# Softmax maxima transposed in place, and a new order of all engines, in a four-layer decode kernel

## The chip, the cores and the metric

The kernel runs on one core of a Trainium2 chip. The metric is the device time of one execution in microseconds (us). Lower is better.

## What is computed

Eight sequences (B = 8) decode one token each. Four layers follow one another: attention (A), MLP (B), attention, MLP, each with a layernorm ahead and a residual sum behind. Both attention layers use the same weights and the same cache.

```python
def _A_ref(x, k_cache, v_cache, wq, wo):         # Hq 16, Hkv 8, Dh 256
    q = (x @ wq).reshape(B, Sq, Hq, Dh)          # D = 448
    k, v = the last W = 1024 rows of each cache, each head used by two query heads
    scores = einsum("bhqd,bhkd->bhqk", q, k) * Dh ** -0.5
    return (einsum("bhqk,bhkd->bhqd", softmax(scores), v)) @ wo
def _B_ref(x, w1, w2):                           # F = 1792
    return silu(x @ w1) @ w2
x = A_x
x = x + _A_ref(_layernorm(x), A_k_cache, A_v_cache, A_wq, A_wo)
x = x + _B_ref(_layernorm(x), B_w1, B_w2)
x = x + _A_ref(_layernorm(x), A_k_cache, A_v_cache, A_wq, A_wo)
x = x + _B_ref(_layernorm(x), B_w1, B_w2)
```

K and V of a sequence are 8 blocks of 512 KB each, so 8.4 MB per sequence and 67 MB in all. The weights add some 10 MB.

## The kernel before

**Work.** A "batch" b is one sequence. `layer1(b)` is its first attention ("layer 0" in the names: S0, PV0). `layer2(b)` is `chain(b)` (layernorm, w1, tanh, w2, fold, layernorm, wq, query blocks) and then its second attention ("layer 1": S1, PV1). The wo of the second attention and the last MLP are done for all eight batches at once, in `final_wo` and `final_rows`.

**Scores and softmax.** A K block that has landed is transposed in place by VectorE, in 32-bit words, two instructions for each slot (L947). `scores` makes 64 matmuls for half the heads (k2 = 0 or 1), and a VectorE reduction (L650) leaves the negated maxima in column k2 of `mseg`. `softmax` combines the maxima of a group of 32 partitions: a transpose (L656), a minimum (L657), and a transpose back (L660) into the same memory as `mseg`, which is called `mb` there. ScalarE makes the exponentials (L664) with these as bias. TensorE transposes them (L669), ScalarE copies them (L673), and the P V products follow (L701, and L731 for the last head of layer 0). Before the change the first transpose wrote `mT`, one tile for both layers. `mseg`, `mg` and `mb` exist once for each layer.

**Slots.** 30 slots of 512 KB hold K and V blocks in turn; a batch takes 16 of them. A K slot comes free when S1 of its half is done, a V slot when PV1 has used it. `pump` adds the loads in the order K 0 to 7, V 0 to 7, batch after batch, all on the SP queue (L471 for K, L477 and L483 for V). Load i reuses the slot of load i - 30: V blocks 6 and 7 of batch b take the slots of K blocks 0 and 1 of batch b - 1.

**Order.** `add` records each task with the keys that it reads and writes. A task that writes a key depends on the last writer and on all readers since, in the order in which the program adds the tasks. `schedule` then makes one fixed order for each engine. A task's urgency is its rank, the length of the remaining path in us by the planner's costs, plus a bias for its kind:

```python
part = "e" if prio < 0 or prio >= 9000 else "abc"[(prio % 100 >= 60) + (prio % 100 >= 70)]
self.kind = ".".join([eng, *(p for i, p in enumerate(name.split(".")) if i != 1), part])
urgency = [t.rank + BIAS.get(t.kind, 0.0) for t in tasks]
sooner = [u for u in can if urgency[u.idx] > urgency[t.idx] and at(u) < now + HOLD * occ[t.idx]]
```

So "pe.S0.1.a" is the second half of layer 0's scores, ".a" is `layer1`, ".b" is `chain` with S1, ".c" is the second attention's softmax and all after it, and ".e" is the start and `final_rows`. `HOLD` says how long an engine is held for a more urgent task that isn't ready yet; `PE_SCALE` multiplies the costs of TensorE tasks. At run time each engine takes its instructions in this order, with semaphore waits where a dependency crosses engines.

**Fillers.** `keep` (L777) and `idle` (L784) are matmuls with zero weights, added to a bank without changing it.

Of the kernel before, what the change touches and what calls it, by code (L numbers as in the profile page):

```python
# [5 lines left out]
F32 = mybir.dt.float32  # L6
U32 = mybir.dt.uint32
ALU = mybir.AluOpType
ACTF = mybir.ActivationFunctionType
AX = mybir.AxisListType  # L10
# [12 lines left out]
       "act:exp": 0.38, "act:oev": 0.30, "act:pTev": 0.20, "act:qrow": 0.51, "act:rowb": 0.50, "act:tanh": 0.22,  # L23
       "pool:pow": 0.53, "pool:pow8": 1.63}
SP_ISSUE, DMA_FIRST, DMA_LAST = 0.47, 1.2, 2.2
HOLD, PE_SCALE = 0.837, 1.062
BIAS = {"dve..e": -51.1, "pe.qsel1.a": -37.9, "pe.S0.0.a": -128.5, "act.exp.a": -58.6, "pe.l.a": 18.8, "act..a":
        -106.8, "act.oev.a": -58.1, "pe.oT.a": 43.2, "pe.wo.a": -42.9, "pe.stat.b": 263.8, "pe.qturn.b": 188.6,
        "pe.qsel.b": 262.3, "dve.max.b": 218.8, "dve.mT.c": 118.3, "dve.mg.c": 108.3, "dve.mb.c": 87.2,
        "act.pTev.c": -93.6, "act.oev.c": -59.6, "pe.oT.c": -79.9, "pe.PV1.1.0.c": -83.7, "pe.PV1.1.2.c":  # L30
        -139.0, "pe.PV1.1.3.c": -36.7, "pe.wo8.c": -95.5, "pe.idle.e": -7.4, "dve.nm8.e": -11.1, "pe.xres.e":
        -10.8}


class Task:
# [13 lines left out]
class Plan:  # L49
# [10 lines left out]
    def add(self, eng, fns, reads=(), writes=(), dur=0.1, prio=0.0, name="", n_bytes=0, dma_key=None):  # L60
        if not isinstance(fns, (list, tuple)):
            fns = [fns]
        if eng == "pool":
            writes = list(writes) + ["pool_serial"]
        t = Task(eng, list(fns), dur, prio, name, n_bytes)
        t.idx = len(self.tasks)
        t.sem = dma_key
        deps = {}

        def dep(o, raw):  # L70
            if o is not t:
                deps[o.idx] = (o, raw or (deps[o.idx][1] if o.idx in deps else False))

        for k in reads:
            if k in self.last_w:
                dep(self.last_w[k], True)
            if k[0] == "bank":
                for r in self.readers.get(k, ()):
                    if r.eng != eng:
                        dep(r, False)  # L80
        for k in writes:
            if k in self.last_w:
                dep(self.last_w[k], True)
            for r in self.readers.get(k, ()):
                dep(r, False)
        for k in reads:
            if k not in writes:
                self.readers.setdefault(k, []).append(t)
        for k in writes:
            self.last_w[k] = t  # L90
            self.readers[k] = []
        t.deps = deps
        self.tasks.append(t)
        return t

    def schedule(self):
# [15 lines left out]
        for t in reversed(tasks):  # L112
            r = max([u.rank + lag(t, u, raw) for u, raw in succ[t.idx]], default=0.0)
            t.rank = occ[t.idx] + r
            if t.eng == "sp":
                t.rank += DMA_FIRST + DMA_LAST
                if t.idx in following:
                    t.rank = max(t.rank, occ[t.idx] + following[t.idx].rank)
        urgency = [t.rank + BIAS.get(t.kind, 0.0) for t in tasks]

# [132 lines left out]
def bass_interleave_layers__sliding_block_cached__dense_activation_silu__decode_kernel(  # L253
# [9 lines left out]
    P = 128  # L263
# [15 lines left out]
    sb = nc.alloc_sbuf_tensor  # L279
# [18 lines left out]
    e_sb = [qbd[i][:].rearrange("p (a b) c d -> p a (b c d)", a=2).rearrange("p a (u n) -> p a u n", u=2) for i in range(2)]  # L298
    pT_sb = [sb(f"pT_sb{i}", [P, 4, 32], BF16) for i in range(2)]
    mseg = [sb(f"mseg{i}", [P, 32], F32) for i in range(2)]  # L300
    mT = [sb("mT", [P, 32], F32)] * 2
    mg = [sb(f"mg{i}", [P, 2], F32) for i in range(2)]
    mb = mseg
    l_sb = [sb(f"l_sb{i}", [P, H], F32) for i in range(2)]
# [42 lines left out]
    def bk(i):  # L347
        return [("bank", i)]
# [4 lines left out]
    def dve(fn, reads, writes, dur, prio, name=""):  # L353
        add("dve", fn, reads=reads, writes=writes, dur=max(0.06, dur - LAT["dve"]), prio=prio, name=name)

    def act(fn, reads, writes, dur, prio, name=""):
        add("act", fn, reads=reads, writes=writes, dur=dur - LAT["act"], prio=prio, name=name)

    def pe(fns, reads, writes, shape, prio, name=""):

        n = len(fns) if isinstance(fns, (list, tuple)) else 1
        add("pe", fns, reads=reads, writes=writes, dur=n * max(0.0265, shape[0] / shape[1] / 2230.0), prio=prio,
            name=name)
# [289 lines left out]

    def softmax(b, layer, prio):
        sc, lb, ei = SC[layer], LB[layer], layer
        dve(lambda e: e.transpose(mT[ei][:], mseg[ei][:]), [("mseg", ei), ("mseg", ei, 0), ("mseg", ei, 1)], ["mT"], 0.21, prio, "mT")  # L656
        dve(lambda e: e.tensor_reduce(  # L657
            mg[ei][:], mT[ei][:, 0:8].rearrange("p (q r) -> p r q", r=2), AX.X, ALU.min),
            ["mT"], [("mg", ei), "mT"], 0.16, prio, "mg")
        dve(lambda e: e.transpose(mb[ei][:].rearrange("p (q r) -> p q r", r=2),  # L660
                                  mg[ei][:].unsqueeze(1).broadcast_to([P, 16, 2])),
            [("mg", ei)], [("mseg", ei), ("mseg", ei, 0), ("mseg", ei, 1)], 0.19, prio, "mb")
        for k2 in range(2):
            act(lambda e, k2=k2: e.activation(  # L664
                e_sb[ei][:, k2, :, :].rearrange("p uh (jj ul) -> p uh jj ul", ul=4),
                bank[sc][:, k2 * 256:(k2 + 1) * 256].rearrange("p (ul uh jj) -> p uh jj ul", ul=4, uh=2),
                ACTF.Exp, bias=mb[ei][:, k2:k2 + 1], scale=1.0),
                bk(sc) + [("mseg", ei, k2)], [("qbd", ei, k2)], 0.5, prio, "exp")
        pe([lambda e, c=c: e.matmul(  # L669
            bank[lb][:].bitcast(BF16)[:, c * P:(c + 1) * P], e_sb[ei][:, c // 2, c % 2, :], ident[:, :],  # L670
            is_transpose=True, start=True, stop=True) for c in range(4)],
           [("qbd", ei, 0), ("qbd", ei, 1), "ident"], bk(lb), (P, 1), prio, "pT")
        act(lambda e: e.activation(  # L673
            pT_sb[ei][:].rearrange("p c (j r) -> p c j r", j=4),
            bank[lb][:].bitcast(BF16)[:, 0:512].rearrange("p (c j r) -> p c j r", c=4, j=4)[:, :, :, 0:8], ACTF.Copy),
            bk(lb), [("pT", ei)], 0.3, prio, "pTev")
        pe([lambda e, uh=uh: e.matmul(  # L677
            bank[lb][:, C_L:C_L + 64], ones_b,
            pT_sb[ei][:].rearrange("p (k uh) n -> p uh k n", uh=2)[:, uh, :, :],
            start=(uh == 0), stop=(uh == 1)) for uh in range(2)],  # L680
           [("pT", ei), "ones_b"], bk(lb), (64, 1), prio, "l")
        dve(lambda e: e.tensor_reduce(  # L682
            l_sb[ei][:], bank[lb][:, C_L:C_L + 64].rearrange("p (n q r) -> p n r q", q=4, r=2), AX.X, ALU.add),
            bk(lb), [("l", ei), ("rl", ei)], 0.23, prio, "lsum")
        dve(lambda e: e.reciprocal(rl_sb[ei][:], l_sb[ei][:]), [("l", ei)], [("l", ei), ("rl", ei)], 0.25, prio, "rl")
# [252 lines left out]
    def layer1(b):  # L938
        prio = 100 * b + 50
        qi = 0  # L940
        if b == 0:
            q_blocks1(0, prio - 45)
        for k in range(8):
            s = slot_of[b, "k", k]
            for h in range(2):
                v = slots[s][:, h * 1024:(h + 1) * 1024].bitcast(U32)
                dve(lambda e, v=v: e.transpose(v, v), [("slot", s)], [("slot", s)], 0.67, prio, "KT")  # L947
        for k2 in range(2):
            scores(b, 0, qi, k2, prio)
        softmax(b, 0, prio)  # L950
        x_init(b, prio)
        if b == 0:
            row_sums(w2_sb, "w2", [(0, 4), (4, 7), (7, 11), (11, 14)], 40)
            row_sums(wo_sb, "wo", [(0, 5), (5, 8), (8, 13), (13, 16), (16, 21), (21, 24), (24, 29), (29, 32)], 40)
        pv_rows(b, 0, 0, prio, oT1, "oT1")
        if b > 0:
            idle(4, prio, "s1", XB)
        wo_part(b, (0, 1), 7, prio + 1)
        wo_part(b, (2, 3), 7, prio + 1)
        pv_rows(b, 0, 1, prio, oT1, "oT1", 3)  # L960
        wo_part(b, (4, 5, 6), 7, prio)
        pv_cols(b, 0, 7, prio, oT1, "oT1")
        wo_part(b, (7,), 7, prio)
        fold(prio, 1.0, [])
        if b + 1 < NB:
            q_blocks1(b + 1, prio + 1)

    def layer2(b):
        prio = 100 * b + 60
        chain(b, prio)  # L970
        for k2 in range(2):
            scores(b, 1, 1, k2, prio + (0.5 if k2 == 0 else 1))
            freed.update((b, "k", 4 * k2 + j) for j in range(4))
            pump()
        prio = 100 * b + 170
        softmax(b, 1, prio)
        if b == NB - 1:
            idle(5, prio, "s1", SC[0])
        for k2 in range(2):
            pv_rows(b, 1, k2, prio + 2, oT2[:, :, :, b], ("oT2", b))  # L980
            freed.update((b, "v", 4 * k2 + q) for q in range(4))
            pump()
            if b == NB - 1:
                final_wo(k2, prio + 3)
# [37 lines left out]
```

## Time and profile before

| | |
|---|---|
| median of 13 runs | 259.0 us (257.02 to 262.48) |
| the profiled execution | 258.75 us, of which its span is 256.5 us |
| busy in the span | PE 191.2, PEld 102.3, DVE 152.6, ACT 88.3, POOL 11.8 us |
| queue of all loads (q1) | 77.68 MB in 50192 packets |
| granted TensorE clock | 0.967 (mean) |

The span goes from the first to the last instruction of the program. PE is TensorE's matmuls, PEld its weight loads, which overlap them; DVE is VectorE, ACT ScalarE, POOL GpSimd, and SP the engine that issues the loads. A busy PE is not PE at its peak, and a DMA engine that is busy need not move data at its full rate.

### The profile page before, as it was taken

The page shows a single profiled execution, that of the slowest core. Times are in us where ns is not written, and L with a number is a line of the kernel's source. Part 1 is how long each engine was busy: PE and PEld are TensorE (multiplying, and loading weights), DVE is VectorE, ACT ScalarE, POOL GpSimd, SP SyncE. Part 2 cuts the span into 40 slices and gives each one's busy share as a digit, 9 for nine tenths or more (in the row PEclk, how much of TensorE's full clock was granted, in tenths as well). Part 3 has the DMA queues.
Part 4 walks back from the last instruction along what each step waited for, and adds up shares of the span by engine and source line. Part 5 has one row for each costly group of instructions (what it writes and reads, how often), then busy time and mean ns, then how long its engine had stood idle before and what let it go on. Part 6 is the DMA issues. An engine that isn't in the chain of part 4 may idle for free.

```text
span 256.5 us, 8596 instructions
## 1 busy us (share of the span) xinstructions
PE 191.2 (75%) x3820; PEld 102.3 (40%) x3820; DVE 152.6 (59%) x416; ACT 88.3 (34%) x241; POOL 11.8 (5%) x25
## 2 busy tenths in 40 slices
PE   0050241388869888998799799979987899798796
PEld 0050120043445345545444454545454445443453
DVE  6448675916872895587488548647853785221322
ACT  2000374815223523432453235334424431423112
POOL 1200000000000000000000000000000000000000
PEclk9999995569999999999999999999999999999999
DMA  6999999999999999999999899989999998300000
GB/s 232 355 383 380 297 341 347 348 362 396 374 350 390 401 351 360 406 375 329 388 406 350 290 403 388 348 245 399 383 324 319 414 360 275 118 3 0 3 3 4
DMA packets 50228, 78.22 MB, mean 305 GB/s; under 512 B 2304, under 2 KB 41104, under 8 KB 49808
## 3 DMA queue, kind: packets, MB, share of 16 engines
q1 hardware_dynamic: 50192, 77.68, 87.1%
q8 instruction: 30, 0.49, 0.8%
q14 instruction: 6, 0.05, 0.1%
HBM read 77.67 MB, written 0.01 MB: 303 GB/s over the span
## 4 chain that ended last, share of the span: by engine, by line
PE 48%; SPq 20%; DMA 13%; DVE 8%; ACT 6%; issue 2%; POOL 0%; ACTq 0%; DVEq 0%
DMA slot<-in_A_k_cache_dram 13%; PE bank L643 11%; PE bank L701 8%; SPq L483 6%; PE bank L818 5%; SPq L433 5%; PE bank L777 4%; PE bank L770 4%; SPq L471 3%; SPq L477 3%; ACT qbd L664 3%; DVE mseg L650 3%; PE bank L805 2%; DVE slot L947 2%; PE bank L521 2%
## 5 line engine op out<-in xcount | busy, mean ns | idle before, releaser
L947 DVE STREAM_TRANSPOSE slot<-slot 128x512 uint32<-128x512 uint32 x128 | 82.4, 686 | 13.5 <-DMA slot<-in_A_k_cache_dram 13.2
L701 PE MATMUL bank<-slot,pT_sb 128*2 128x256 bf16 x960 | 38.2, 279 | 9.5 <-DMA slot<-in_A_v_cache_dram 9.1
L643 PE MATMUL bank<-slot,qbd 128*8 128x256 bf16 x1024 | 39.4, 282 | 4.8 <-DVE mseg L650 2.5
L701 PEld LDWEIGHTS bank<-slot,pT_sb 128*2 128x2 bf16 x960 | 20.4, 83 | 18.6 <-DMA slot<-in_A_v_cache_dram 9.0
L664 ACT ACTIVATE qbd<-bank,mseg 128x256 bf16<-128x256 f32 x32 | 13.0, 473 | 41.6 <-DVE mseg L660 22.4
L643 PEld LDWEIGHTS bank<-slot,qbd 128*8 128x8 bf16 x1024 | 21.0, 85 | 13.1 <-DVE mseg L650 4.5
L709 ACT ACTIVATE qbd<-bank 128x256 bf16<-128x256 f32 x32 | 12.3, 384 | 24.7 <-PE bank L701 18.9
L612 ACT ACTIVATE qbd<-bank,mask 128x128 bf16<-128x128 f32 x32 | 12.1, 378 | 24.8 <-PE bank L607 23.6
L770 PE MATMUL bank<-wo_sb,oT 128*1 128x449 bf16 x256 | 19.6, 359 | 0.0
L777 PE MATMUL bank<-wq_sb,cols_b 128*128 128x512 bf16 x64 | 19.4, 384 | 0.0
L755 POOL TENSOR_TENSOR rhalf<-var,nhalf 128x1 f32<-128x1 f32 x16 | 8.8, 550 | 217.0 <-ACT var L753 217.0
L650 DVE TENSOR_REDUCE mseg<-bank 128x1 f32<-128x256 f32 x32 | 12.9, 414 | 8.6 <-PE bank L643 8.3
L818 PE MATMUL bank<-wq_sb,xbt 128*1 128x512 bf16 x256 | 16.6, 378 | 0.6 <-DVE xbt L744 0.6
L669 PE MATMUL bank<-ident,qbd 128*128 128x128 bf16 x64 | 6.4, 222 | 13.8 <-ACT qbd L664 13.8
L715 DVE TENSOR_TENSOR oT<-bank,l_sb 128x16 bf16<-128x16 f32 (+1 forms) x32 | 5.9, 199 | 16.7 <-PE bank L711 16.3
L682 DVE TENSOR_REDUCE l_sb<-bank 128x16 f32<-128x64 f32 x16 | 3.2, 201 | 19.3 <-PE bank L677 19.3
L784 PE MATMUL bank<-wq_sb,cols_b 128*128 128x512 bf16 x49 | 13.5, 382 | 0.0
L825 ACT ACTIVATE qrow<-bank 128x512 bf16<-128x512 f32 x16 | 9.6, 597 | 9.1 <-PE bank L818 9.1
L669 PEld LDWEIGHTS bank<-ident,qbd 128*128 128x128 bf16 x64 | 3.6, 98 | 19.2 <-ACT qbd L664 19.2
L452 DVE TENSOR_REDUCE qbd<-wo_sb 128x5 f32<-128x2240 bf16 x4 | 9.7, 2480 | 2.6 <-DMA wo_sb<-in_A_wo_dram 2.6
L626 DVE TENSOR_TENSOR qbd<-bank,maskr 128x256 bf16<-128x256 f32 x16 | 6.8, 424 | 6.8 <-PE bank L621 6.7
L790 ACT ACTIVATE qrow<-bank 128x449 bf16<-128x449 f32 x8 | 4.4, 550 | 17.7 <-PE bank L770 17.7
(146 smaller groups left out, 214.4 us busy)
## 6 DMA issues: line engine op xcount, KB each, us to landing
slot<-in_A_k_cache_dram SPq DMA_DIRECT2D x64, 512.0 KB, 10.6
slot<-in_A_v_cache_dram SPq DMA_DIRECT2D x64, 512.0 KB, 8.8
wo_sb<-in_A_wo_dram SPq DMA_DIRECT2D x1, 3584.0 KB, 17.8
wq_sb<-in_A_wq_dram SPq DMA_DIRECT2D x3, 1024.0 KB, 7.1
w_sb<-in_B_w_dram SPq DMA_DIRECT2D x4, 336.0 KB, 16.2
w_sb<-in_B_w_dram SPq DMA_DIRECT2D x1, 1344.0 KB, 11.3
wq_sb<-in_A_wq_dram SPq DMA_DIRECT2D x2, 256.0 KB, 10.5
w_sb<-in_B_w_dram SPq DMA_DIRECT2D x4, 112.0 KB, 9.4
```

Of the source, the lines that this page charges most:

```text
L433: dma(lambda e, j=j: e.dma_start(rows[:, 3 * j:3 * j + 3, :], parts[j, 0:3 * P, :].rearrange("(c p) n -> p c n", p=P)), [("w2", j)], 3 * P ...
L483: dma(lambda e: e.dma_start(slots[s][:, :].rearrange("v (j n) -> v j n", j=4), src.rearrange("j (v uh) d -> v j (uh d)", uh=2)), [("slot", ...
L643: fns.append(lambda e, cb=cb, par=par, j=j, kvh=kvh, kv=kv: e.matmul(bank[sc][32 * j:32 * j + 8, k2 * 256:(k2 + 1) * 256], qbd[qi][:, kvh, ...
L650: dve(lambda e: e.tensor_reduce(mseg[layer][:, k2:k2 + 1], bank[sc][:, k2 * 256:(k2 + 1) * 256], AX.X, ALU.max, negate=True), bk(sc), [("m ...
L664: act(lambda e, k2=k2: e.activation(e_sb[ei][:, k2, :, :].rearrange("p uh (jj ul) -> p uh jj ul", ul=4), bank[sc][:, k2 * 256:(k2 + 1) * 2 ...
L701: fns.append(lambda e, q=q, uh=uh, j=j, vv=vv: e.matmul(bank[ob][32 * j:32 * j + 2, c0:c0 + DH], pT_sb[ei][:, k2 * 2 + uh, j * 8 + 2 * q:j ...
L709: act(lambda e: e.activation(o_t, bank[ob][:, c0:c0 + DH], ACTF.Copy), bk(ob), [("qbd", ei, k2)], 0.42, prio, "oev")
L770: fns.append(lambda e, i=i, c=c, kvh=kvh: e.matmul(bank[XB][32 * c:32 * c + 1, 0:D1], oT1[:, i % 2, i // 2:i // 2 + 1], wo_sb[:, i * DP:i ...
L777: pe([lambda e: e.matmul(bank[SC[1]][:], zero_b.broadcast_to([P, P]), wq_sb[:, 0:512], start=False, stop=True, skip_group_check=True) for ...
L784: pe(lambda e: e.matmul(bank[bi][:], zero_b.broadcast_to([P, P]), wq_sb[:, 0:512], start=False, stop=True, skip_group_check=True), [("wq", ...
L818: pe([lambda e, j=j, c=c, k2=k2, wb=wb: e.matmul(bank[wb][32 * j:32 * j + 1, :], xbt[:, xcol(c, k2):xcol(c, k2) + 1], wq_sb[:, c * HD + (( ...
L947: dve(lambda e, v=v: e.transpose(v, v), [("slot", s)], [("slot", s)], 0.67, prio, "KT")
```

## The change

The tile `mT` is gone. The first transpose of `softmax` works in place in `mseg[ei]`, the minimum reads it there, and the second transpose writes back into it as it did before. All three carry the keys of their own layer's `mseg`, so no key is shared by the softmaxes of the two layers. The constants that shape the order of all engines are new.

```diff
-HOLD, PE_SCALE = 0.837, 1.062
-BIAS = {"dve..e": -51.1, "pe.qsel1.a": -37.9, "pe.S0.0.a": -128.5, "act.exp.a": -58.6, "pe.l.a": 18.8, "act..a":
-        -106.8, "act.oev.a": -58.1, "pe.oT.a": 43.2, "pe.wo.a": -42.9, "pe.stat.b": 263.8, "pe.qturn.b": 188.6,
-        "pe.qsel.b": 262.3, "dve.max.b": 218.8, "dve.mT.c": 118.3, "dve.mg.c": 108.3, "dve.mb.c": 87.2,
-        "act.pTev.c": -93.6, "act.oev.c": -59.6, "pe.oT.c": -79.9, "pe.PV1.1.0.c": -83.7, "pe.PV1.1.2.c":
-        -139.0, "pe.PV1.1.3.c": -36.7, "pe.wo8.c": -95.5, "pe.idle.e": -7.4, "dve.nm8.e": -11.1, "pe.xres.e":
-        -10.8}
+HOLD, PE_SCALE = 0.435, 1.148
+BIAS = {"pe.S0.0.a": 21.5, "dve.max.a": 23.0, "pe.S0.1.a": 61.5, "dve.mg.a": 3.5, "dve.mb.a": -28.7,
+        "dve.rsum.a": 92.7, "pe.PV0.0.0.a": -48.9, "act.oev.a": -15.0, "dve.oTev.a": 22.4, "dve.xb.b": 37.0,
+        "pe.stat.b": 20.8, "pe.w1.b": 12.9, "pe.keep.b": -26.6, "pe.w2.b": 19.7, "pe.fold.b": 57.4,
+        "pe.qturn.b": 40.0, "pe.qsel.b": 62.1, "pe.S1.0.b": 37.2, "dve.max.b": 26.6, "pe.PV1.0.1.c": -60.2,
+        "pe.PV1.1.0.c": -70.8, "pe.PV1.1.3.c": -28.5, "pe.idle.a": 36.6}
...
-    mT = [sb("mT", [P, 32], F32)] * 2
...
-        dve(lambda e: e.transpose(mT[ei][:], mseg[ei][:]), [("mseg", ei), ("mseg", ei, 0), ("mseg", ei, 1)], ["mT"], 0.21, prio, "mT")
+        M = [("mseg", ei), ("mseg", ei, 0), ("mseg", ei, 1)]
+        dve(lambda e: e.transpose(mseg[ei][:], mseg[ei][:]), M, M, 0.21, prio, "mT")
         dve(lambda e: e.tensor_reduce(
-            mg[ei][:], mT[ei][:, 0:8].rearrange("p (q r) -> p r q", r=2), AX.X, ALU.min),
-            ["mT"], [("mg", ei), "mT"], 0.16, prio, "mg")
+            mg[ei][:], mseg[ei][:, 0:8].rearrange("p (q r) -> p r q", r=2), AX.X, ALU.min), M, [("mg", ei)] + M, 0.16, prio,
+            "mg")
         dve(lambda e: e.transpose(mb[ei][:].rearrange("p (q r) -> p q r", r=2),
                                   mg[ei][:].unsqueeze(1).broadcast_to([P, 16, 2])),
-            [("mg", ei)], [("mseg", ei), ("mseg", ei, 0), ("mseg", ei, 1)], 0.19, prio, "mb")
+            [("mg", ei)], M, 0.19, prio, "mb")
```

## The prediction

> **What bounds the kernel now.** I read the slices of the page first, then the chain, then the waits of the DMA queue, then one batch in the stretches and in the timeline.
>
> ```profile
> DMA  6999999999999999999999899989999998300000
> GB/s 232 355 383 380 297 341 347 348 362 396 374 350 390 401 351 360 406 375 329 388 406 350 290 403 388 348 245 399 383 324 319 414 360 275 118 3 0 3 3 4
> PE 48%; SPq 20%; DMA 13%; DVE 8%; ACT 6%; issue 2%; POOL 0%; ACTq 0%; DVEq 0%
> SPq L477 <- PE bank L643: 28.4, 7, 5.5
> ```
>
> The loads run until slice 34 (about 221 us); then 35 us follow without any. The DMA row says 9 nearly throughout, yet the second line dips once per batch (290, 245, 319) and touches 414: the engines are occupied, not full. The last line says why: seven times the SP queue stood with a V load until score matmuls (L643) gave a slot back.
>
> The trace's landing of each load gives the prices: in a full queue a K load lands 1.28 us after the one before it, a V load 1.47 us. A batch of 8 + 8 therefore costs 8 x 1.28 + 8 x 1.47 = 22.0 us. The first K load of batches 2 to 7 landed at 82.16, 104.24, 127.61, 150.92, 175.32 and 200.19, the last V load at 221.5. From 82.16 the pure stream would need 6 x 22.0 - 1.28 = 130.7 us and end at 212.9; so 8.6 us are lost to slots that come late. Now the loop that makes them late:
>
> ```profile
> 143.90:167.63 23.73, 21.45 (x439) 11.55 (x439) 15.63 (x43) 8.95 (x24) 1.10 (x2) 1.00 1.01 359
> 221.50:256.50 35.00, 30.43 (x588) 15.30 (x580) 8.67 (x40) 9.31 (x24) 1.65 (x3) 1.00 0.01 3
> 143.41 0.75 DVE L650 TENSOR_REDUCE mseg<-bank 128x1 f32<-128x256 f32 x2 [0.17 <-PE bank L643]
> 143.89 1.15 PE L643 MATMUL bank<-slot,qbd 128*8 128x256 bf16 x32 [0.17 <-DVE mseg L650]
> 145.09 0.42 DVE L650 TENSOR_REDUCE mseg<-bank 128x1 f32<-128x256 f32 x1 [0.93 <-PE bank L643]
> 145.55 0.21 DVE L656 STREAM_TRANSPOSE mT<-mseg 128x32 f32<-128x32 f32 x1
> 145.79 0.16 DVE L657 TENSOR_REDUCE mg<-mT 128x2 f32<-128x8 f32 x1
> 145.99 0.21 DVE L660 STREAM_TRANSPOSE mseg<-mg 128x32 f32<-128x32 f32 x1
> 146.12 0.17 DVE L656 STREAM_TRANSPOSE mT<-mseg 128x32 f32<-128x32 f32 x1
> 146.29 1.57 ACT L664 ACTIVATE qbd<-bank,mseg 128x256 bf16<-128x256 f32 x4 [4.82 <-DVE mT L656]
> 149.01 1.48 PE L701 MATMUL bank<-slot,pT_sb 128*2 128x256 bf16 x48
> ```
>
> The first two lines are one steady batch and the tail (columns: PE, PEld, DVE, ACT, POOL busy, clock, DMA share, GB/s). A batch takes 23.73 us at full clock; PE is busy in 21.45 of them, of which 12 fillers (`keep` L777, `idle` L784) hold about 3.0, each counted to the next matmul's start.
>
> In the timeline, the two L650 at 143.41 are the first half of layer 1 of batch 3 and the second half of layer 0 of batch 4: the latter's maxima are complete at 144.16. The matmuls at 143.89 and the L650 at 145.09 are layer 1's second half. Only then comes an L656, and only after its L657 the other L656. In program order `softmax(3, 1)` is added before `softmax(4, 0)`, and both write "mT": the planner must put layer 1's transpose and minimum first. So batch 4 waits from 144.16 to 146.12 for the end of batch 3, and its two exponentials are third and fourth of the four from 146.29. This sits on the loop: softmax(4, 0), P V, wo, both halves of the MLP, wq, scores of layer 1, and again the same.
>
> **What the Trainium skill says.** "PSUM — Partial Sum Buffer", Engine vs sequencer instructions: the queues of ScalarE and VectorE are strict FIFO, and matmuls start and complete in program order. The trace agrees: VectorE has only 0.75 us of work between 143.41 and 145.09 and doesn't take the ready L656. "DMA: Bandwidth & Descriptors", Anatomy of one DMA: the DMA engines wait for no semaphore; the issuing sequencer does. The L477 waits above are that. "Perfetto Trace Analysis", Optimization Strategy: a gap that repeats can mean too few buffers; here 30 slots for 16 loads a batch, and the gap repeats.
>
> **The change, part by part.**
> - *Tile and in-place transpose.* The same three VectorE instructions per softmax, 16 times: 0.21 + 0.16 + 0.21 us; none added, no DMA or POOL work moves. In-place 32-bit transposes already run at L947 (686 ns for 128x512, x128), so I book no difference; bounds, from the 0.17 to 0.21 of L656: -0.04 to +0.04 us each, under 0.7 us in all.
> - *What falls away.* Layer 0's transpose can start at 144.2, its exponential 0.64 us later at 144.9 instead of 147.03 (146.29 plus two exponentials at 0.37): 2.1 us. The transposes (L669), P V of layer 0 at 149.01 and wo after it move by the same, or more if the score matmuls of the next batch are put earlier. That shortens the loop from 23.73 to about 21.6.
> - *What is late next.* The stream at 22.0 us a batch, and PE. The V loads 6 and 7 also form a loop: V7 of batch 5 was issued at 167.55, when S1 of batch 4 freed its slot, landed at 174.06, and the column P V needing it began at 176.57, 14.3 us before the next S1 half ended. That is 6.5 + 14.3 = 20.8 without slack, under the stream. PE has 21.45 us of work per batch; its busiest share in any batch stretch is 91%. At 95% the period is 22.6 us. I take 22.6: bounds 22.0 (the stream) and 23.6 (21.45 at 91%).
> - *The new order* (HOLD 0.837 to 0.435, PE_SCALE, BIAS). A bias is in us of remaining path, and one batch is 23.7. S0.1 gets +61.5 and S0.0 goes from -128.5 to +21.5: scores of the next layer 0 come before most of chain(b), whose steps carry 12.9 to 62.1. PV1.1 stays negative (-28.5 to -70.8), PV0.0.0 gets -48.9: these fill PE's gaps. That uses the new freedom; its cost is in the rivals. Unshown by the trace: I book zero apart from the period, bounds -1 to +1 us a batch. The tail's own biases (`.e`) go: 30.43 of 35.00 us are busy PE there, so zero, bounds -0.7 to +0.7.
> - *Sum.* Six batch steps from batch 1's to batch 7's layer-1 scores. Five at 23.7 - 22.6 = 1.1 make 5.5; the last, without loads to wait for, gets 1.0, half of the 2.1. The tail from V7 of batch 7 on keeps its length, as its P V (221.21) already started within 0.3 us of the last landing. 6.5 us off the profiled time of 258.75 (span 256.5 + 2.25 around it) is 252.25; the median of the 13 runs is 0.25 higher: **252.4**.
> - *Ends.* All 8.6 us of the stream, plus 1.0 in the last step: 249.4; with the small terms (0.6 and 0.7) on the good side 248. At 23.6 a batch, with the last step's 1.0: 257.4.
>
> **Rivals.**
> 1. *PE crowded (slower).* What may now be queued ahead of chain(b): S0.1 (1.1 us), the transposes (0.4), P V of layer 0 (1.8), four `idle` (1.0): 4.3 us. PE is FIFO; if a score group at the head waits for a late K transpose (L947 waited 13.2 us for loads in all), fold, w1, w2 and wq stand behind it, and behind S1 the SP queue. The slack from 20.8 to 23.73 is 2.9 us; above that the kernel gets slower. With 3.8 of it in the way, 0.9 x 6 = 5.4 us: 264. For it: 21.45 busy of 23.73. Against: S0 is already interleaved with the chain, and 3.0 us are fillers.
> 2. *Slots, not softmax (no change).* If the new order leaves S1's first half no earlier, V6 and V7 land as before, only 2.5 us (174.06 to 176.57) before they are needed, and the gain is eaten: 258.9. For it: that thin margin. Against: S1 follows the loop that gets shorter.
> 3. *The freedom is not used.* If VectorE's new order still has layer 1's softmax first, the time is 258.8. `mb` of layer 0 at -28.7 and the missing lift of layer 1's steps speak for and against.
>
> **How the numbers follow.** About 0.3% is what a measurement of this kernel can tell from no change: 258.2 to 259.8. Main case, 248 to 254.5: 0.50; a part of it, 254.5 to 258.2: 0.17; rivals 2 and 3: 0.08; rival 1, from 259.8 to 268: 0.25. Range: 5% lies below 248 and some 14% of rival 1 above 262.
>
> **What would show it.** Right: an L656 and its L660 well before layer 1's last L650 of the batch, layer 0's exponentials apart from layer 1's; batch stretches of 22 to 23 us; first K landings 22.0 to 22.8 apart; no slice under 320 GB/s between 59 and 210 us; the last V load at 213 to 217. Wrong: stretches of 24 us or more with PE waiting at L643 for VectorE's slot transposes (rival 1), or V loads still issued one S1 late with the softmaxes apart (rival 2).

## The result, and the profile after

| | before | changed |
|---|---|---|
| median | 259.36 us (48 runs) | 254.2 us (11 runs, 252.61 to 256.48) |
| the profiled execution | 258.75, span 256.5 | 255.35, span 253.5 |
| mean granted clock in it | 0.967 | 0.979 |

The ratio is 0.9803, with a 95% interval of 0.9777 to 0.983: about 5 us less. The two profiled spans differ by only 3.0 us; the changed one's profile is 1.15 us above its median. In this text a *step* is the time from the end of the first half of layer 1's scores of one batch to the same point of the next. (A correction to the description above: the scores of one half are 32 matmuls, not 64; both halves together are 64.)

From the page of the changed kernel, the slices (clock, DMA share, bandwidth):

```profile
PEclk9999999999777999999999999999999999999999
DMA  6999999999999999999999999999999999100000
GB/s 227 366 389 380 308 342 348 348 371 393 376 350 386 378 322 319 393 392 349 355 407 373 337 377 408 349 356 402 384 339 381 398 354 320 57 3 3 0 3 5
```

And its chain by engine:

```profile
PE 55%; SPq 16%; DMA 9%; DVE 8%; ACT 6%; issue 3%; POOL 0%; ACTq 0%; DVEq 0%
```

The dips of the GB/s line to 290 and 245 are gone, the last V load lands at 217.83 us instead of 221.5, and more of the chain is PE (55%, 48% before). A second profile of the same kernel, reported below, is less clear in both: one slice at 279 GB/s, and 50% of the chain on PE. The clock line shows what I hadn't reckoned with: slices 11 to 13 run below full clock.

One batch in the timeline of the changed kernel, with VectorE, ScalarE and TensorE in one list (start, us, engine, line, operation):

```profile
142.05 0.42 DVE L648 TENSOR_REDUCE mseg<-bank 128x1 f32<-128x256 f32 x1 [0.62 <-PE bank L641]
142.51 0.21 DVE L655 STREAM_TRANSPOSE mseg<-mseg 128x32 f32<-128x32 f32 x1
142.76 0.16 DVE L656 TENSOR_REDUCE mg<-mseg 128x2 f32<-128x8 f32 x1
...
142.96 0.21 DVE L659 STREAM_TRANSPOSE mseg<-mg 128x32 f32<-128x32 f32 x1
...
143.26 0.84 ACT L663 ACTIVATE qbd<-bank,mseg 128x256 bf16<-128x256 f32 x2 [1.83 <-DVE mseg L659]
...
144.16 0.40 PE L668 MATMUL bank<-ident,qbd 128*128 128x128 bf16 x4 [0.29 <-ACT qbd L663]
...
144.48 1.09 PE L641 MATMUL bank<-slot,qbd 128*8 128x256 bf16 x32
...
145.63 0.42 DVE L648 TENSOR_REDUCE mseg<-bank 128x1 f32<-128x256 f32 x1 [1.30 <-PE bank L641]
146.08 0.21 DVE L655 STREAM_TRANSPOSE mseg<-mseg 128x32 f32<-128x32 f32 x1
...
146.53 1.04 PE L700 MATMUL bank<-slot,pT_sb 128*2 128x256 bf16 x32
...
146.83 0.84 ACT L663 ACTIVATE qbd<-bank,mseg 128x256 bf16<-128x256 f32 x2 [1.96 <-DVE mseg L659]
```

Layer 0 of batch 4 has its last maximum at 142.47 and is transposed at once (142.51). Its exponentials are finished before the last score matmuls of batch 3's layer 1 (144.48) begin. Layer 0's first P V of batch 4 follows the end of those by 0.96 us; before the change it was 3.98. Layer 1's own softmax starts later, at 146.08, and nothing waits for it. The in-place transpose takes 0.21 us in all 16 cases.

The steps of the changed kernel from batch 3 to 4 and from 5 to 6 (columns as in the prediction):

```profile
142.94:165.07 22.13, 21.16 (x440) 11.62 (x440) 15.95 (x42) 9.12 (x24) 1.10 (x2) 1.00 1.05 370
...
188.01:211.87 23.86, 21.26 (x441) 11.76 (x441) 15.89 (x42) 9.24 (x24) 1.10 (x2) 1.00 1.05 370
```

PE's work per step is nearly what it was, 21.2 us, in 22.13 us instead of 23.7: 96% busy. The second stretch is the worst of the six. The mean of the six is 22.66 us here and 22.90 in the second profile, so one profile gives a step to about a quarter of a microsecond.

TensorE's own waits show what the tie cost. Both lines are of the window from 143 to 165 us, the first before the change and the second after it (who waited for whom; us in total, times, longest):

```profile
PE bank L669 <- ACT qbd L664: 1.5, 2, 1.2
PE bank L668 <- ACT qbd L663: 0.3, 1, 0.3
```

Over the six steps TensorE stood 0.9 to 1.5 us for the exponentials before and stands 0.3 to 0.4 us now: in the mean 1.0 us less, where the step is 1.2 us shorter. The 3.98 us between the scores and layer 0's first P V were thus mostly not idle. Fillers, two groups of transposes and some of layer 1's P V stood in them, and this work is now elsewhere in the step.

**Where the 3.0 us of the two profiles come from**, by the same four points in both traces:

| stretch | before | changed | difference |
|---|---|---|---|
| start to batch 1's first S1 half | 95.69 | 98.02 | +2.33 |
| six steps to batch 7's | 143.12 | 135.94 | -7.18 |
| from there to the last VectorE operation | 15.86 | 16.55 | +0.69 |
| writing the output, to the end | 1.86 | 2.97 | +1.11 |

### The profile page after: what moved, and what is told of

It reads as the page before. It is cut to its first block, busy times and chain, and to the rows that moved or that the text cites. A ratio compares the mean times of both kernels' runs of the same rounds, so it can differ in the third digit from the quotient of the medians.

```text
span 253.5 us, 8598 instructions
## 1 busy us (share of the span) xinstructions
PE 194.2 (77%) x3820; PEld 104.6 (41%) x3820; DVE 153.4 (61%) x416; ACT 89.1 (35%) x241; POOL 11.8 (5%) x25
## 4 chain that ended last, share of the span: by engine, by line
PE 55%; SPq 16%; DMA 9%; DVE 8%; ACT 6%; issue 3%; POOL 0%; ACTq 0%; DVEq 0%
PE bank L641 11%; PE bank L700 10%; SPq L481 6%; PE bank L817 6%; DMA slot<-in_A_v_cache_dram 6%; PE bank L769 5%; SPq L431 5%; PE bank L776 4%; DMA slot<-in_A_k_cache_dram 4%; ACT qbd L663 3%; PE bank L804 2%; DVE mseg L648 2%; PE bank L519 2%; DVE slot L946 2%; SPq L469 2%
## 5 line engine op out<-in xcount | busy, mean ns | idle before, releaser
L946 DVE STREAM_TRANSPOSE slot<-slot 128x512 uint32<-128x512 uint32 x128 | 83.8, 690 | 6.7 <-DMA slot<-in_A_k_cache_dram 5.9
L700 PE MATMUL bank<-slot,pT_sb 128*2 128x256 bf16 x960 | 39.7, 279 | 12.7 <-DMA slot<-in_A_v_cache_dram 10.0
L641 PE MATMUL bank<-slot,qbd 128*8 128x256 bf16 x1024 | 40.9, 299 | 8.6 <-DVE slot L946 6.1
L641 PEld LDWEIGHTS bank<-slot,qbd 128*8 128x8 bf16 x1024 | 25.9, 89 | 15.8 <-DVE slot L946 6.7
L700 PEld LDWEIGHTS bank<-slot,pT_sb 128*2 128x2 bf16 x960 | 19.6, 82 | 22.8 <-DMA slot<-in_A_v_cache_dram 9.3
L776 PE MATMUL bank<-wq_sb,cols_b 128*128 128x512 bf16 x64 | 19.2, 381 | 0.0
L769 PE MATMUL bank<-wo_sb,oT 128*1 128x449 bf16 x256 | 17.6, 365 | 0.0
L783 PE MATMUL bank<-wq_sb,cols_b 128*128 128x512 bf16 x49 | 14.3, 402 | 0.0
L668 PEld LDWEIGHTS bank<-ident,qbd 128*128 128x128 bf16 x64 | 4.0, 103 | 13.6 <-ACT qbd L663 12.8
L710 PEld LDWEIGHTS bank<-ident,qbd 128*128 128x128 bf16 x64 | 3.7, 98 | 12.2 <-ACT qbd L708 6.4
```

The costliest lines, as they stand in the source:

```text
L641: fns.append(lambda e, cb=cb, par=par, j=j, kvh=kvh, kv=kv: e.matmul(bank[sc][32 * j:32 * j + 8, k2 * 256:(k2 + 1) * 256], qbd[qi][:, kvh, ...
L700: fns.append(lambda e, q=q, uh=uh, j=j, vv=vv: e.matmul(bank[ob][32 * j:32 * j + 2, c0:c0 + DH], pT_sb[ei][:, k2 * 2 + uh, j * 8 + 2 * q:j ...
L769: fns.append(lambda e, i=i, c=c, kvh=kvh: e.matmul(bank[XB][32 * c:32 * c + 1, 0:D1], oT1[:, i % 2, i // 2:i // 2 + 1], wo_sb[:, i * DP:i ...
L776: pe([lambda e: e.matmul(bank[SC[1]][:], zero_b.broadcast_to([P, P]), wq_sb[:, 0:512], start=False, stop=True, skip_group_check=True) for ...
L783: pe(lambda e: e.matmul(bank[bi][:], zero_b.broadcast_to([P, P]), wq_sb[:, 0:512], start=False, stop=True, skip_group_check=True), [("wq", ...
```

## The experiments

Each kernel below says what it changes against the kernel before or the changed one. Steps are means of the six.

| kernel | median us | ratio to before, interval | step | layer 0's first P V after the end of the last S1 |
|---|---|---|---|---|
| before | 259.36 | | 23.85 | 3.98 |
| changed | 254.2 | 0.9803 (0.9777 to 0.983) | 22.66 | 0.96 |
| changed, again | 254.58 | 0.9778 (0.9703 to 0.9853) | 22.90 | 0.96 |
| tile alone | 257.17 | 0.993 (0.9901 to 0.9959) | 23.30 | 1.7 to 2.1, later 3.97 |
| order alone | 271.68 | 1.0502 (1.045 to 1.0555) | 25.50 | 3.52 |
| changed, late softmax | 283.32 | 1.0952 (1.0875 to 1.103) | 27.03 | 5.23 |
| changed, half of V | 250.5 | 0.9684 (0.9616 to 0.9751) | 22.19 | 0.96 |
| before, half of V | 258.87 | one run | 23.88 | 3.95 |

### The tile alone

The changed kernel with HOLD, PE_SCALE and BIAS of the kernel before.

```diff
-HOLD, PE_SCALE = 0.435, 1.148
+HOLD, PE_SCALE = 0.837, 1.062
...
```

> The tile change alone: the transpose in place with each layer's own keys, and HOLD, PE_SCALE and BIAS of the kernel before, so that the order is worked out anew by the old numbers. Theory A (the shared tile holds layer 0's softmax behind layer 1's; freed, the batch step falls from 23.85 to about 22.7 us): the old numbers let layer 0's softmax go first in some batches only, so a part of the gain, 255.5 to 257.5 us, with steps of 22.7 to 23.4 where layer 0's first transpose comes before layer 1's last maximum. Theory B (the new order brings the gain by itself, the tile little): 258.5 to 260.

Measured 257.17 us, inside A's span and below B's. The trace splits into two halves. For batches 2, 3 and 4 the old numbers let layer 0's softmax go first, and the three steps that hold it are 22.71, 22.87 and 23.28. For batches 5, 6 and 7 layer 1's comes first again, the P V of layer 0 starts 3.97 us after S1 as before, and the steps are 23.72, 23.76 and 23.44. The windows of one step of either sort in this kernel:

```profile
121.71:144.58 22.87, 20.82 (x442) 11.76 (x441) 15.46 (x42) 9.08 (x24) 1.10 (x2) 1.00 1.06 372
...
191.58:215.34 23.76, 20.60 (x443) 11.89 (x441) 15.88 (x42) 8.94 (x24) 1.10 (x2) 1.00 1.01 350
```

PE has the same work in both (20.82 and 20.60 us busy); the slow one only waits longer. For the exponentials it stands 0.2 us in the first and 1.5 us in the second, as in the kernel before. This is the cleanest of the runs: one kernel and one execution, with and without the late softmax.

### The order alone

The kernel before, with its shared mT, and HOLD, PE_SCALE and BIAS of the changed kernel.

```diff
-HOLD, PE_SCALE = 0.837, 1.062
+HOLD, PE_SCALE = 0.435, 1.148
...
```

> The new HOLD, PE_SCALE and BIAS alone, with the tile mT shared as before. Theory A: layer 1's transpose and minimum have to come first again, the step goes back to 23.7 or more, 259 to 262 us (the new numbers were not made for this order). Theory B: 254 to 256, as the changed kernel.

Measured 271.68 us: B falls, and A was too mild. With the shared tile the new numbers are 5% slower than the old ones. The P V of layer 0 comes 3.52 us after S1, and the step is 25.5. In the step from 150.35 to 175.31 us TensorE waits 1.6 us for the exponentials, as before, but its other waits add up to 2.3 us, against 0.7 in the kernel before. These numbers were made for the free tile; whether some other order could beat the old one with the shared tile wasn't tried.

### The changed kernel with the late softmax

The order of the changed kernel is kept, and in it layer 0's softmax is moved behind layer 1's. The edit does one thing more: on TensorE the transposes of both layers' exponentials go directly behind S1, where layer 1's had stood after layer 0's first P V and the fillers had come first. So it is harsher than what the shared tile forces.

```diff
         self.order["sp"] = loads
+        for b in range(7):
+            for e, names in (("dve", ("mT", "mg", "mb")), ("act", ("exp", "pTev")), ("pe", ("pT",))):
+                o = self.order[e]
+                first = [t for t in o if t.name in names and t.name != "pTev" and t.prio == 100 * b + 170]
+                then = [t for t in o if t.name in names and t.prio == 100 * b + 150]
+                o[:] = [t for t in o if t not in then and (e != "pe" or t not in first)]
+                if e == "pe":
+                    k = max(i for i, t in enumerate(o) if t.name == "S1.%d.1" % b) + 1
+                    o[k:k] = first + then
+                else:
+                    k = o.index(first[-1]) + 1
+                    o[k:k] = then
```

> The changed kernel with one thing put back: in every batch step layer 0's transposes, minimum, exponentials, their transposes and copy stand behind those of layer 1, as the shared tile forced it; all else keeps the new order. Theory A: the 2.1 us of the prediction come back on the loop in each of six steps, less what slack the loop has: step 23.5 to 24.2, 258 to 262 us. Theory B: within 1 us of the changed kernel, 253.5 to 255.5.

Measured 283.32 us: the direction is A's, the size is not. One batch in its timeline (TensorE and ScalarE; lines are 12 higher than in the changed kernel):

```profile
181.13 1.05 PE L653 MATMUL bank<-slot,qbd 128*8 128x256 bf16 x32 [0.52 <-DVE qbd L636]
...
183.45 1.57 ACT L675 ACTIVATE qbd<-bank,mseg 128x256 bf16<-128x256 f32 x4 [5.19 <-DVE mseg L667]
...
184.34 1.34 PE L680 MATMUL bank<-ident,qbd 128*128 128x128 bf16 x8 [2.15 <-ACT qbd L675]
...
185.90 1.48 PE L795 MATMUL bank<-wq_sb,cols_b 128*128 128x512 bf16 x3 [0.22 <-issue]
...
187.42 1.02 PE L712 MATMUL bank<-slot,pT_sb 128*2 128x256 bf16 x16
```

PE stands 2.15 us for the exponentials, and the fillers (L795) that hid in this place now come after them. The first P V is 4.27 us later against S1's end than in the changed kernel (5.23 - 0.96), and the step is 4.37 us longer (27.03 - 22.66). The two numbers agree better than they should, for something else moves too. After each such wait the granted clock is low:

```profile
185.00:190.00 5.00, 4.13 (x47) 2.22 (x51) 0.48 (x2) 0.84 (x4) 0.00 (x0) 0.51 1.03 405
```

(The window of the same kernel from 185 to 190 us; 0.51 is the clock.) The 32 matmuls of layer 0's first P V take 1.88 us here and 1.04 in the changed kernel. Over the step from 179.76 to 206.79 us PE is busy for 22.62 us, at a mean clock of 0.87, instead of some 21.2, and it waits 2.2 us for the exponentials instead of 0.3. So of the 4.37 us about 1.4 are the clock and 1.9 the wait; the rest are shorter waits around it. The run shows that a late softmax lengthens the step, but not what the shared tile alone costs.

One reading of the table is tempting and wrong. Step less the last column is 19.9 us in the kernel before, and 21.7 to 22.0 in those with the new order, as if that order had put some 2 us more into the rest of the loop. With half of V, where no load is late, it is 19.9 and 21.2. But some 2.5 us of PE work stood between S1 and the first P V before the change (144.97 to 149.01 us), and about 1 us does after it, so most of the difference is work that has changed its place.

### Half of each V block

From batch 2 on only the first half of each V block is loaded; source and both forms of load_v are cut in the same way.

```diff
+        nv = 4 if b < 2 else 2
...
-            dma(lambda e: e.dma_start(slots[s][:, :].rearrange("v (q n) -> v q n", q=4),
+            dma(lambda e: e.dma_start(slots[s][:, :].rearrange("v (q n) -> v q n", q=4)[:, 0:nv, :],
...
```

In the changed kernel:

> The changed kernel with only half of each V block loaded from batch 2 on (the other half of the slot keeps old data; same instructions and order otherwise). It tells what is late next. If the stream of loads binds (22.0 us a batch): the steps fall by several us and the time to 240 or less. If PE and the chain bind: steps stay at 22.0 to 22.6 and the time is 251 to 254. My sum had the second, with the stream 0.6 us behind.

In the kernel before:

> The kernel before with only half of each V block loaded from batch 2 on (the other half of the slot keeps old data). Theory A (the loop through the tied softmaxes sets the step of 23.85 us, the loads do not): 256 to 259 us, steps of 23.3 to 23.8, against 250.5 us and steps of 22.2 of the changed kernel with the same cut. Rival 2 (late V loads set the step): steps fall by a us or more, 252 or less.

Measured 250.5 us (two runs) and 258.87 us (one run; a second one of 425.45 was disturbed and is left out). One step of the changed kernel with half of V, from batch 4 to 5 (windows):

```profile
162.38:184.54 22.16, 20.64 (x437) 11.74 (x441) 15.81 (x42) 9.13 (x24) 1.10 (x2) 1.00 0.81 288
```

One of the kernel before with half of V, from batch 3 to 4:

```profile
143.37:167.04 23.67, 21.41 (x445) 11.54 (x437) 15.66 (x42) 8.94 (x24) 1.10 (x2) 1.00 0.77 269
```

With the DMA engines down to some 80% the kernel before keeps its step to within 0.1 us: it wasn't bound by loads, and rival 2 falls. That the tied softmaxes were the bound is what the tile alone shows. The changed kernel's six steps become even, 22.11 to 22.37, and the mean falls by 0.47 (0.71 against the second profile). So its compute loop takes about 22.2 us, and late loads add the other half microsecond or so, most of it in the 22.94 and 23.86.

### Fillers: all of them, those of batch 1, and xres

Four of the ten runs ask about the fillers, the start and the tail. First the changed kernel again, unedited, as their neighbour on one chip:

> The changed kernel again, as the neighbour of the next three on the same chip: 253 to 255.5 us. If the low clock of slices 11 to 13 is of the kernel and not of one run, this profile shows the clock below 9 somewhere between 65 and 110 us again; if it was a freak, not.

Measured 254.58 us. The clock is below 9 in slices 11 to 13 once more, so the place of the dip is that of the first profile. Batch 1's S1 half ends at 98.01 us, 98.02 in the first. The steps are 23.52, 22.78, 22.84, 22.65, 23.17 and 22.41.

Then without any idle matmuls in the batches:

```diff
-        if b > 0:
-            idle(4, prio, "s1", XB)
```

> The changed kernel without the four idle matmuls of every batch; order worked out anew. Rival 1 (PE is crowded, fillers are in the way): each of six steps loses up to their 1.0 us, so 248 to 252. Theory D (the fillers stand where PE would wait anyhow for the exponentials): 253 to 255.5. If the fillers are what keeps the clock up, the clock falls below 9 in the steady stretch and the time is 256 or more.

Measured 255.28 us, ratio 0.9849 (0.9773 to 0.9924), a step of 23.06. A microsecond of PE work per batch less doesn't shorten the step. The order was worked out anew, and in it wo comes ahead of the second half of P V, so this isn't a clean test of the fillers' price; but they don't stand in the way. The clock stayed full in the steady stretch.

Without those of batch 1 alone:

```diff
-        if b > 0:
+        if b > 1:
             idle(4, prio, "s1", XB)
```

> The changed kernel without the four idle matmuls of batch 1 (they stand ahead of that batch's transposed exponentials at 76.8 to 78.7 us of its profile; the later batches keep theirs). Theory A (the fillers in PE's queue hold up the first P V, and the whole pipeline after it): batch 1's P V and wo come 1 to 2 us earlier, and 0.5 to 2 us of the whole follow, 252 to 253.7 us. Theory C (the start is limited by the loads and slot transposes, and a lost start is caught up later): within 0.5 us of the changed kernel.

Measured 254.66 us, beside 254.58. Batch 1's first P V is 2.67 us earlier (77.02, not 79.69), yet its S1 half ends at 97.97, not 98.01. C holds in this profile: what is won there is lost by 98 us, in slices that again run at a low clock (0.50 from 75 to 80 us).

The same, and xres behind yturn:

```diff
-               ["xbt8", "nm8", "back_b", "ident"], bk(bi), (P, 1), prio - 0.1, "xres")
+               ["xbt8", "nm8", "back_b", "ident", "turned"], bk(bi), (P, 1), prio - 0.1, "xres")
```

> As the kernel without the idle matmuls of batch 1, and in the last MLP the two residual groups (xres) stand behind the transposes of the hidden row (yturn) again, as in the kernel before. Theory A: 0.3 us less than that kernel, from 246.54 to 246.85 us of the changed kernel's profile, where xres keeps yturn waiting. Theory C: no difference that shows.

Measured 253.28 us, ratio 0.9748 (0.9694 to 0.9802). From the hidden row's evacuation to yturn it takes 0.58 us instead of 0.93: 0.35 less, where 0.3 was expected. The start is that of the run before, but here batch 1's S1 half ends at 96.98 us, with less of a dip (0.88, 0.50 and 0.94 in the three windows from 70 to 85 us, where the run before had 0.77, 0.50 and 0.70). The median is lower than that of the changed kernel's second measurement by 1.3 us, but its runs had the better clock: at 0.986 or 0.987 the mean of three is 253.9 us, against 254.3 for five of the changed kernel's first measurement (254.6 with a sixth at 256.48); at 0.993 it is 252.7 against 253.2. That leaves some half a microsecond for both edits, and the interval overlaps with that of the changed kernel. It is the fastest complete version measured, not one proven faster than the changed kernel.

### Fillers in the wait

The kernel of the last run, with so many zero matmuls behind each of the named steps of batch 0 in TensorE's order.

```diff
     pl.schedule()
+    spots = (("S0.0.1", 12), ("l", 10), ("PV0.0.0.0", 3), ("PV0.0.0.1", 3), ("PV0.0.0.2", 3), ("PV0.0.0.3", 4), ("oT", 2))
...
```

> As the kernel without the idle matmuls of batch 1 and with xres behind yturn, and 37 filler matmuls put into PE's queue between 30 and 52 us, where it waits for V and for weights. If the low clock between 65 and 110 us comes from PE going from nearly idle to dense work at 52 us: it moves to the wait or goes, and the time falls by 0.5 to 1.5 us, to 252 to 253. If it has another cause: the low slices stay where they are, 253 to 254.5 us; the fillers cost under 0.3.

Measured 253.41 us, ratio 0.9767 (0.9669 to 0.9865). The clock line of its page:

```profile
PEclk9999997999965999999999999999999999999999
```

The low slices 12 and 13 stay, and a new one comes in slice 7, where the fillers are. That PE's step from idle to dense work causes this dip isn't supported.

### What the low clock costs

Every execution has a mean granted clock on record, and it changes from one to the next. The 12 of the changed kernel: 255.92 us at 0.973, 255.35 at 0.979 (the profiled one), 253.73 to 256.48 in six at 0.986 or 0.987, 252.61 to 254.2 in three at 0.993, 253.46 at 1.0. By these few runs a dip costs this kernel some 2 us when it is deep, about 1 us in a middling run. Of the 37 of the kernel before that have one, the 11 at 0.96 to 0.967 have a mean of 258.6 us, the 21 at 0.993 or 1.0 of 259.6: there a dip of that size costs nothing, though five others, at 0.954 and 0.98 to 0.987, took 261.2 to 263.4. The clock line of the kernel before shows the reason for the 0.967 of its profile:

```profile
PEclk9999995569999999999999999999999999999999
```

Slices 7 to 9 are 38 to 58 us, where PE has little work and waits for loads. The kernel before with half of V has no dip there in its profile, a clock of 1.00 from 35 to 60 us, and its batch 1 reaches the same point at 95.66 us, against 95.69. In the changed kernel the low slices are 11 to 13, 63 to 82 us, under batch 1's scores and the end of batch 0. Its half-V twin has the same order and the same loads up to batch 2; its profiled execution has a clock of 1.00 from 70 to 80 us where the changed kernel has 0.73 and 0.59 (both have 0.66 from 65 to 70), and batch 1's S1 half ends at 95.65, not 98.02. Two groups of 32 score matmuls in this stretch, from 72.01 and from 74.98 us, take 1.69 and 1.88 us in the changed kernel; the same two take 1.12 and 1.11 in the twin. So the +2.33 of the first row is the low clock of that execution.

## Why the prediction was right, and where it was off

- **The false dependency was the bound: right.** Under the old numbers the free tile shortens just those steps in which it is used, and in them TensorE's wait for the exponentials falls from 1.5 to 0.2 us. Under the new numbers the shared tile keeps that wait at 1.6 us, and the kernel gets slower. The late softmax put back makes the step 4.37 us longer, but the clock and a moved group of transposes have a share in that.
- **The step: right in size, 22.6 forecast, 22.66 measured, 22.90 in the second profile.** The six steps gave 7.18 us where the sum had 6.5. That the first profile meets the 22.6 so closely is partly luck. PE reaches 96% in a good step, so the 95% was fair; but the compute loop alone is 22.2, and the rest are late loads, which the sum had counted as hidden. The 2.1 us by which the exponentials come earlier didn't pass to the step whole: TensorE had stood idle for about 1.0 us of them only, and the limit that the sum set by PE's work was the one that held.
- **The sum has a slip of 0.1 us:** 252.25 and 0.25 make 252.5, and the upper end by the same terms is 257.5.
- **The loads as the present bound: wrong.** The first part read the 8.6 us that the stream loses as the price of late slots. They are lost, but as a consequence: with half of V the kernel before keeps its 23.9. The line of the SP queue that it went by wasn't even the largest: before it in the same view stands L483 with 35.8 us in six waits. The waits didn't get shorter, either. In the changed kernel the line that answers to the one shown of before is

```profile
SPq L475 <- PE bank L827: 27.3, 7, 6.0
```

  27.3 us in seven waits, against 28.4. In the kernel before with half of V, whose step is unchanged, it is 43.3 us. A long wait of the queue says that it runs ahead of the slots, not that loads come late.
- **The start: a missing term, +2.33 us in the profile.** The sum began at batch 1's scores and had nothing before them. A low clock fell on work there. At a clock of 0.993 or 1.0 the changed kernel takes 252.6 to 254.2 us; its median is at 0.986. So of the 1.8 us from 252.4 to 254.2 about 0.9 is this (the mean of those four is 253.3), and the tail below holds the rest.
- **The tail: booked at zero within 0.7, measured +0.69.** xres ahead of yturn is 0.35 of it; the wo of the last attention starts 0.2 us later, and its evacuation another 0.2. The output's last write took 1.11 us more in this profile, which I had no term for. It is 1.86 or 2.97 us in the traces here (about 2.97 in both of the changed kernel, its half-V twin and the one with the late softmax, about 1.86 in all others); I haven't found why.
- **The in-place transpose at no cost: right,** 0.21 us, x16.
- **Rival 1, PE crowded: its place was right in part, its sign not.** At 72.01 us of the changed profile a group of batch 1's scores goes ahead of batch 0's query blocks, whose input is ready at the same moment and which start at 73.63. That is its mechanism, but in the six steps it doesn't outweigh the gain: PE's waits add up to about 8 us there, and to about 14 before. With the shared tile the new order does lose, by other waits of 2.3 us in a step instead of 0.7: that is the 271.68.
- **Rival 3, freedom not used:** it is the second half of the run with the tile alone.
- **What would show it.** Layer 0's transposes and exponentials lie as described. Five of six steps are between 22 and 23 (four of six in the second profile). The first K loads land 22.05 to 24.1 us apart, one slice has 319 GB/s, and the last V load at 217.83 is just past the 217. The late start and the two steps with late loads are the likely reasons; no run separates them.

## What to carry to other kernels

A scratch tile shared by two stages costs nothing in memory traffic, but it fixes the order of the stages. Look for the pair of instructions that could run and don't, and ask whether they sit on the loop that repeats. Then remove the tie and find the order anew together: here each alone gave -0.7% and +5%, and both gave -2%. A delay in the timeline is worth only what the busiest engine stands idle in it: layer 0's first P V moved 3.0 us closer to the scores, and the step lost 1.2. To tell whether loads bind, make them smaller; their queue's waits don't tell.

## What the hardware showed that I had not expected

In every profile the granted clock fell to between 0.5 and 0.9 for 5 to 25 us, at one or two places in all but the kernel with the late softmax. It fell between 63 and 85 us in the changed kernel (twice), without the fillers of batch 1 (with xres moved, too) and with fillers in the wait; at 75 to 80 us without any batch fillers; at 35 to 58 us in the kernel before; in both places with the tile alone; at 90 to 105 and 205 to 210 us with the order alone; at 65 to 70 us in the changed kernel with half of V, at 220 to 225 in the kernel before with it.

The two profiles of the changed kernel agree in place and depth: 0.66, 0.73 and 0.59, then 0.66, 0.72 and 0.60, from 65 to 80 us. But the mean clock of its 12 executions goes from 0.973 to 1.0, so the dip isn't the same in all. Nor does the program with its idle time decide it. The kernel before and its half-V twin run the same instructions with the same loads up to batch 2. From 40 to 50 us PE is busy for 2.4 us in both, and the clock is 0.50 in one profile and 1.00 in the other.

Whether a dip costs anything is a matter of what PE has to do there: up to 2.4 us, or nothing. Zero matmuls in PE's idle time from 30 to 50 us didn't take the dip away and brought a second one (0.69 from 35 to 40 us). The late softmax, with 2.15 us of idle PE and the fillers only behind it, has a dip after every wait. These don't give one rule, and what causes the dips stays open.
